# An attention kernel fused with a feed-forward layer: where batch index 0 forms phi's products for batch index 1

## The chip, the cores and the metric

The kernel runs on one core of a Trainium2 chip. The metric is device time in microseconds (us); all times without a unit are microseconds. TensorE (PE) multiplies matrices, VectorE (DVE) and ScalarE (ACT) do the elementwise work, and SyncE (SP) issues nearly all transfers (DMAs). PEld in the profile is PE's loading of weights, which overlaps its multiplying.

## The reference

Eight batches, eight heads, 576 tokens, head size 64, and 32 memory slots per head:

```python
a = phi - np.max(phi, axis=2, keepdims=True)
a = np.exp(a)
a = a / (np.sum(a, axis=2, keepdims=True) + 1e-09)
k_m = np.einsum('bhsm,bhsd->bhmd', a, k)
v_m = np.einsum('bhsm,bhsd->bhmd', a, v)
scores = scale * np.matmul(q, k_m.transpose(0, 1, 3, 2))
attn = softmax(scores)                  # over the 32 memory slots
x = np.matmul(attn, v_m)                # to (tokens, 512)
h = x @ w_in                            # 512 -> 2048
g = h * (1.0 / (1.0 + np.exp(-h)))
out = g @ w_out                         # 2048 -> 512
```

## The kernel before

**Stages of one batch.** The phi logits are reduced to their maximum, subtracted and exponentiated. `e_mm` (L325) multiplies them with a tile that holds k, v and a column of ones: four chunks of 128 tokens (L335, 32 products) and one of 64 (L345, 8 products). These are *phi's products*. Their result is 129 columns wide in two banks of PSUM, one per half of the heads. Behind them DVE adds an epsilon to the sums (L353) and inverts them (L355), and ACT (L359) and DVE (L361) write the scaled k_m and v_m, `kvn`. PE transposes that (`e_tr`, L367), makes the scores (`s_mm`, L400), and DVE and ACT do the softmax. x is never formed: `p_mm` (L649) multiplies v_m into w_in and gives *P*, and the FFN's first product is attention times P. In batch index 0, P is made in eight blocks of 256 columns; the sixth is `j == 5`. `p_split` (L677 on ACT, L679 on DVE) stores each block of P as a high and a low part.

**The FFN.** Batch indices 0 and 1 run 16 *slots*, one for each 128 columns of the hidden layer (L1300). In a slot, `ffn1` (L701, twelve products, high and low parts) writes h, two banks with 288 used columns each. ACT applies silu: L728 takes 512 tokens into `gbuf`, L730 the 64 others into `gleft`. DVE splits the result into high (L718) and low (L720) parts. Then PE does the second FFN product of the slot before, `main_step` (L746): four token tiles of three products each, into four accumulating banks. In batch index 0 the tiles go in two halves, and small steps ("events") stand behind each half: those of slot 8 behind tiles 0 and 1, those of slot 8.5 behind tiles 2 and 3.

**PSUM.** Eight banks: four accumulate (`acc`), two hold h, and two are the tile `bg`. Both have one buffer, so a new h or a new bg waits until all readers of the last are done. P's blocks and the scores use bg. Of h only columns 0 to 287 of each bank are used by the FFN; `beside_h` (L216) hands out columns from 288 on of the h in use.

**What sets the order.** PE's and SP's instructions stay in the order of the code. On ACT and DVE the framework orders batch index 0; the code adds that ACT's part of an event stands behind the last L730 (L1321). Each engine works its row strictly in order. Batch index 0 also converts the weights, from 64-bit words as they are loaded into the parts that the products need: per block of w_in or w_out, L172, L174 and L180 on ACT, and L176, L178 and L182 on DVE (`w_conv`). SP loads one block whenever another is done.

Of the kernel before, what the change touches and what calls it, by code (L numbers as in the profile page):

```python
# [23 lines left out]
KVW = 2 * D + 1  # L24
DMODEL, DFF = 512, 2048
NFC = DFF // P
CW = 256
# [21 lines left out]
def attn_ffn_kernel(  # L49
# [65 lines left out]
    def bgtile():  # L115
        return ps.tile([P, 2, 512], F32, tag="bg", name="bg", bufs=1)
# [90 lines left out]
    at = [dict() for _ in range(B)]  # L207
    live = {}

    def banks(b):  # L210
        if b == 0:
            return [ps.tile([P, 512], F32, tag="acc", name=f"first{i}", bufs=NI) for i in range(2)]
        bg = bgtile()
        return [bg[:, 0], bg[:, 1]]

    def beside_h(w):  # L216

        return [live["h"][:, i, HALF : HALF + w] for i in range(2)]
# [29 lines left out]
    def rows(p):  # L248
        return slice(REST * p, REST * (p + 1))
# [75 lines left out]
    def e_mm(b, cs=range(FULLC)):  # L325
        e, er, kvt, kr = (at[b][k] for k in ("e", "er", "kv", "kr"))
        if cs[0] == 0:
            at[b]["pt"] = beside_h(KVW) if b and b % 2 == 0 else banks(b)
        pt = at[b]["pt"]
        turns = [(c, p) for c in cs for p in range(2)]  # L330
        if b == 0:
            turns.sort(key=lambda t: t[1])
        for c, p in turns:
            for r in range(NR):
                nc.tensor.matmul(  # L335
                    pt[p][M * r : M * (r + 1), :KVW],
                    e[:, p, c, M * r : M * (r + 1)],
                    kvt[c][:, p, r],
                    start=c == 0, stop=False, skip_group_check=True,
                )  # L340
        if cs[-1] != FULLC - 1:
            return
        for r in range(NR):
            for p in range(2):
                nc.tensor.matmul(  # L345
                    pt[p][M * r : M * (r + 1), :KVW],
                    er[rows(p), M * r : M * (r + 1)],
                    kr[rows(p), r],
                    start=False, stop=True, skip_group_check=True,
                )  # L350
        rs = [sb.tile([P, 1], F32, tag="rs", name="rs", bufs=2) for p in range(2)]
        for p in range(2):
            nc.vector.tensor_scalar(rs[p], pt[p][:, 2 * D : KVW], EPS, None, op0=ALU.add)  # L353
        for p in range(2):
            nc.vector.reciprocal(rs[p], rs[p])  # L355
        for p in range(2):
            src = pt[p][:, : 2 * D].rearrange("p (k d) -> p k d", k=2)
            if p == (b == 0):
                nc.scalar.activation(kvn[:, :, p], src, AF.Copy, scale=rs[p])  # L359
            else:  # L360
                last_kvn[:] = [nc.vector.tensor_scalar(kvn[:, :, p], src, rs[p], None, op0=ALU.mult)]  # L361
# [656 lines left out]
    def ev(b, slot, fn, *a):  # L1018
        events.setdefault((b, slot), []).append((fn, a))

    def steady(b, n):


        early = b > 2
        if not early:
            ev(b, 1, phi_max, n)
            for i in range(3):
                ev(b, 2, phi_fold, n, i)
            ev(b, 3, phi_sub, n)
        ex = exp_slots(b)[0]  # L1030
        em = ex + 1 + b % 2
        ev(b, ex, phi_exp, n)
        ev(b, em, e_mm, n)
        for hf in range(2):
            ev(b, em + 1, load_q, n, hf)
        ev(b, ex + 4, e_tr, n)
        ev(b, ex + 5, s_all, n)
        ev(b, 9 if early else 10, s_max, n, ALL)
        ev(b, 10, s_sub, n, ALL)
        ev(b, 11, s_exp, n, ALL)  # L1040
        ev(b, 12 if early else 11, s_sum, n, ALL)
        ev(b, 13 if early else 12, s_norm, n, FIRST)
        turn = NFC + 3 if b % 2 else 14 if early else 13
        ev(b, turn, s_back, n, FIRST)
        ev(b, turn, s_high, n, FIRST)
        ev(b, turn, s_low, n, FIRST)
        for k in range(3):
            ev(b, 10 + 2 * k, win_load, n, k)
        if b % 2:
            ev(b, NFC, win_load, n, 3)  # L1050
        for k in range(2):
            ev(b, NFC + 2 if b % 2 else 13 + k, p_mm, n, k * JW, JW, True, b % 2 and k)
        m = n + 1
        if m < B:
            ev(b, ex + 3, load_kv, m, range(2))
            ev(b, ex + 3, load_phi, m)
            ev(b, ex + 6, load_kv, m, range(2, FULLC))
            ev(b, 7 if early else 14, phi_max, m)
            for i in range(3):
                ev(*((b, 11 + i) if early else (b + i // 2, (14, 15, 0)[i])), phi_fold, m, i, load)  # L1060
            ev(b + 1, 1, phi_sub, m)

    for b in range(B):
        n = b + 1
        if b == 0:
            for j in range(2, DFF // CW):
                ev(b, 2 * j - 1.5, p_mm, b, j * CW, CW)
        elif b == 1:
            ev(b, 0, win_save)
            for j in range(1, NJ):  # L1070
                ev(b, 4 * j - 3, p_mm, b, j * JW, JW)
            for j in range(NP):
                ev(b, 1.5 * j + 2, w_forms, j, 0)
                ev(b, 1.5 * j + 2.5, w_forms, j, 1)
        else:
            pair = b > 2 and b % 2 == 0
            if not pair:
                ev(b, 0, win_load, b, 3)
            ev(b, 0 if b > 2 else 1, p_mm, b, 2 * JW, JW)
            if b > 2:  # L1080
                ev(b, 3, s_norm, b, SECOND)
                for fn in (s_back, s_high, s_low):
                    ev(b, 4 + b % 2, fn, b, SECOND)
            late = b % 2 and 2 < b < B - 1
            ev(b, 0 if pair else 4 if late else 2, p_mm, b, 3 * JW, JW, not late, pair)
            if n < B:
                steady(b, n)
            if late:
                ev(b, 4, p_rest, b, 3 * JW)
            continue  # L1090
        at_slot = (
            (4, 5, 6, 7.5, 9, 9.5, 11.5, 12.5, 13, 13.5, 14, 14) if b == 0
            else (1, 2, 3, 5, 9, 10, 10, 11, 12, 13, 13, 14)
        )
        mx, sub, ex, em, tr, s0, s1, sx, se, ss, sn, sk = at_slot
        ev(b, mx, phi_max, n)
        if n == 1:
            ev(b, sub, phi_allmax, n, (0, 1), (0,))
            ev(b, sub + 0.5, phi_allmax, n, (0, 1), (1,))
        else:  # L1100
            for i in range(3):
                ev(b, sub, phi_fold, n, i)
        ev(b, sub + 0.5, phi_sub, n)
        ev(b, ex, phi_exp, n)
        ev(b, em, e_mm, n)
        ev(b, 14 if b == 0 else em + 1, load_kv, n + 1, range(FULLC if b == 0 else 2))
        ev(b, tr, e_tr, n)
        ev(b, em, load_q, n, 1)
        if n == 1:
            ev(b, s0, s_mm, n, 0)  # L1110
            ev(b, s1, s_mm, n, 1)
        else:
            ev(b, s0, s_all, n)
        if b == 0:
            ev(b, s1, load_q, n + 1, 0)
        else:
            ev(b, s1 + 1, load_kv, n + 1, range(2, FULLC))
        ev(b, sx, s_max, n, ALL)
        ev(b, sx, s_sub, n, ALL)
        ev(b, se, s_exp, n, ALL)  # L1120
        ev(b, ss, s_sum, n, ALL)
        ev(b, sn, s_norm, n, ALL)
        for u in (FIRST, SECOND) if n == 1 else (ALL,):
            ev(b, sk, s_back, n, ALL, u)
            ev(b, sk, s_high, n, ALL, u)
        ev(b, sk, s_low, n, ALL)
        ev(b, sk, load_phi, n + 1)
        if b == 0:
            ev(b, 14, p_mm, n, 0, JW)
        else:  # L1130
            for k in range(3):
                ev(b, 12 if k == 2 else 6 + k, win_load, n, k)
            for k in range(2):
                ev(b, 12 + 2 * k, p_mm, n, k * JW, JW)
# [17 lines left out]
    with in_order(DVE, ACT) as last:  # L1152
# [18 lines left out]
        for p in range(2):  # L1171
            phi_exp(0, (p,))
        keep_warm(idle, 2)
        e_mm(0)
        w_conv(I0, 0, "pc")
        keep_warm(idle, 3)
# [112 lines left out]
    for b in range(B):  # L1289
# [3 lines left out]
        for s in range(NFC if b > 1 else 0):  # L1293
            t, j = divmod(s, NP)
# [43 lines left out]
def build(arrays, bacc, num_devices=1):  # L1338
    nc = bacc.Bacc("TRN2", target_bir_lowering=False, num_devices=1, dynamic_dma_scratch_size=1024)
    aps = [  # L1340
        nc.dram_tensor(n, a.shape, mybir.dt.from_np(a.dtype), kind="ExternalInput").ap() for n, a in arrays.items()
    ]
    out = nc.dram_tensor("out", (B * S, DMODEL), F32, kind="ExternalOutput").ap()
    with tile.TileContext(nc) as tc:
        attn_ffn_kernel(tc, *aps, out)
    return nc
# [44 lines left out]
```

## Time and profile before

| | |
|---|---|
| median of 3 runs | 679.05 (678.32 to 679.21) |
| the profiled execution | 678.47, of it span 676.7 |
| PE busy | 667.1 (99%) |
| PE weight loads busy | 588.6 (87%) |
| DVE busy | 518.6 (77%) |
| ACT busy | 368.5 (54%) |
| transfers | 93.92 MB |
| PE's granted clock, mean | 0.999 |

The span runs from the first instruction to the last. The times in rows of the profile count from its start. A row of a timeline has start, duration, engine, line, operation, what it writes and reads, and in brackets how long the engine stood idle ahead of it and what ended that. Matmuls are pipelined: the step from start to start is what one costs, and the duration holds the way through the array too. Batch index 0 ends at about 105 of 676.7.

### The profile page before, as it was taken

The page shows a single profiled execution, that of the slowest core. Times are in us where ns is not written, and L with a number is a line of the kernel's source. Part 1 is how long each engine was busy: PE and PEld are TensorE (multiplying, and loading weights), DVE is VectorE, ACT ScalarE, POOL GpSimd, SP SyncE. Part 2 cuts the span into 40 slices and gives each one's busy share as a digit, 9 for nine tenths or more (in the row PEclk, how much of TensorE's full clock was granted, in tenths as well). Part 3 has the DMA queues.
Part 4 walks back from the last instruction along what each step waited for, and adds up shares of the span by engine and source line. Part 5 has one row for each costly group of instructions (what it writes and reads, how often), then busy time and mean ns, then how long its engine had stood idle before and what let it go on. Part 6 is the DMA issues. An engine that isn't in the chain of part 4 may idle for free.

```text
span 676.7 us, 14541 instructions
## 1 busy us (share of the span) xinstructions
PE 667.1 (99%) x5792; PEld 588.6 (87%) x5792; DVE 518.6 (77%) x1093; ACT 368.5 (54%) x681; POOL 0.7 (0%) x6
## 2 busy tenths in 40 slices
PE   7999999999999999999999999999999999999997
PEld 3577778787888998999988999899997999889996
DVE  4997899988948689868877688877877668867653
ACT  3878684533625556654655546564654546554541
POOL 0000000000000000000000000000000000000000
PEclk9999999999999999999999999999999999999999
DMA  9998975224270552253420535116430204300001
GB/s 340 373 339 276 315 304 192 81 103 146 78 233 22 184 183 100 79 180 124 179 95 16 185 97 179 70 42 237 157 126 32 86 2 156 111 31 17 32 1 47
DMA packets 37907, 93.92 MB, mean 139 GB/s; under 512 B 4688, under 2 KB 21456, under 8 KB 34256
## 3 DMA queue, kind: packets, MB, share of 16 engines
q1 hardware_dynamic: 36816, 90.22, 38.4%
q10 hardware_dynamic: 1024, 2.77, 1.1%
q8 instruction: 46, 0.75, 0.5%
q14 instruction: 21, 0.17, 0.1%
HBM read 77.22 MB, written 15.73 MB: 137 GB/s over the span
## 4 chain that ended last, share of the span: by engine, by line
PE 73%; DVE 10%; issue 2%; ACT 2%; DVEq 0%; ACTq 0%
PE sum L893 35%; PE h L854 22%; PE lsum L977 5%; PE bg L649 3%; PE acc L746 3%; PE h L701 2%; PE accleft L746 2%; DVE gparts L720 1%; PE bg L335 1%; PE bg L382 1%; DVE pm L679 1%; DVE kept L836 1%; DVE gparts L718 1%; DVE smx L426 1%; PE h L335 1%
## 5 line engine op out<-in xcount | busy, mean ns | idle before, releaser
L854 PE MATMUL h<-aparts,pm 128*128 128x288 f32 x1152 | 168.7, 295 | 0.0
L854 PEld LDWEIGHTS h<-aparts,pm 128*128 128x128 f32 x1152 | 157.3, 188 | 0.8
L868 ACT ACTIVATE gbuf<-h 128x512 f32<-128x512 f32 x96 | 57.3, 597 | 117.0 <-PE h L854 113.7
L893 PE MATMUL sum<-wo_hi,aparts 128*128 128x256 f32 x384 | 102.6, 289 | 0.0
L893 PE MATMUL sum<-kept,aparts 128*128 128x256 f32 x576 | 100.1, 282 | 0.0
L893 PE MATMUL sum<-wo_lo,aparts 128*128 128x256 f32 x384 | 100.0, 282 | 0.0
L873 DVE TENSOR_TENSOR gbuf<-gbuf 128x256 f32<-128x256 f32 x96 | 40.5, 422 | 71.4 <-ACT gbuf L868 70.9
L882 ACT ACTIVATE aparts<-gbuf 128x512 fp32r<-128x512 f32 x86 | 54.4, 633 | 63.4 <-DVE gbuf L877 63.4
L746 PE MATMUL acc<-wo_hi,gparts 128*128 128x512 f32 x256 | 85.0, 397 | 0.2
L893 PEld LDWEIGHTS sum<-wo_hi,aparts 128*128 128x128 f32 x384 | 72.8, 189 | 11.5 <-ACT gleft L870 10.1
L893 PEld LDWEIGHTS sum<-kept,aparts 128*128 128x128 f32 x576 | 82.6, 191 | 0.0
L884 DVE TENSOR_TENSOR gparts<-gbuf,aparts 128x512 fp32r<-128x512 f32 x86 | 59.5, 692 | 19.1 <-ACT aparts L882 19.1
L893 PE MATMUL sum<-wo_hi,gparts 128*128 128x256 f32 x384 | 73.2, 281 | 0.0
L893 PEld LDWEIGHTS sum<-wo_lo,aparts 128*128 128x128 f32 x384 | 73.1, 190 | 0.0
L893 PE MATMUL sum<-kept,gparts 128*128 128x256 f32 x288 | 65.5, 282 | 0.0
L746 PEld LDWEIGHTS acc<-wo_hi,gparts 128*128 128x128 f32 x256 | 47.6, 188 | 14.5 <-DVE gparts L720 1.5
L893 PEld LDWEIGHTS sum<-wo_hi,gparts 128*128 128x128 f32 x384 | 59.4, 190 | 0.0
L701 PEld LDWEIGHTS h<-aparts,pm 128*128 128x128 f32 x372 | 51.7, 188 | 6.8 <-issue 3.4
L701 PE MATMUL h<-aparts,pm 128*128 128x288 f32 x372 | 56.0, 299 | 0.6 <-DVE aparts L612 0.5
L872 ACT ACTIVATE aparts<-gbuf 128x384 fp32r<-128x384 f32 x96 | 50.4, 525 | 0.0
L746 PE MATMUL acc<-wo_lo,gparts 128*128 128x512 f32 x128 | 49.3, 393 | 0.4 <-DVE wo_lo L182 0.4
L893 PEld LDWEIGHTS sum<-kept,gparts 128*128 128x128 f32 x288 | 47.9, 190 | 0.0
(225 smaller groups left out, 956.1 us busy)
## 6 DMA issues: line engine op xcount, KB each, us to landing
win<-win_saved SPq DMA_DIRECT2D x24, 1024.0 KB, 5.2
kv<-in_kv SPq DMA_DIRECT2D x28, 516.0 KB, 5.0
q<-in_q SPq DMA_DIRECT2D x16, 576.0 KB, 6.2
raw<-in_w_in SPq DMA_DIRECT2D x14, 512.0 KB, 7.6
raw<-in_w_out SPq DMA_DIRECT2D x6, 1024.0 KB, 6.5
win_saved<-win SPq DMA_DIRECT2D x4, 1024.0 KB, 8.6
phi<-in_phi SPq DMA_DIRECT2D x7, 576.0 KB, 8.3
out<-oo SPq DMA_DIRECT2D x26, 128.0 KB, 2.3
```

The costliest lines, as they stand in the source:

```text
L335: nc.tensor.matmul(pt[p][M * r : M * (r + 1), :KVW], e[:, p, c, M * r : M * (r + 1)], kvt[c][:, p, r], start=c == 0, stop=False, skip_grou ...
L649: nc.tensor.matmul((bg[p][M * r : M * (r + 1)] if beside else bg[M * r : M * (r + 1), p, :w]).rearrange("p (k f) -> p k f", f=P), kvT[D * ...
L701: nc.tensor.matmul(h[:, hf, :HALF], wt[:, p, fs], a[:, p, hf * HALF : (hf + 1) * HALF], start=n[hf] == 0, stop=n[hf] == 5, skip_group_chec ...
L746: nc.tensor.matmul(acc[key], gt[:, cs], wt[:, fc], start=fc == 0 and n == 0, stop=fc == NFC - 1 and n == 2)
L854: nc.tensor.matmul(h[:, i, :HALF], wt[:, p, f : f + P], a[:, p], start=n == 0, stop=n == 5)
L868: nc.scalar.activation(gbuf[:, :MAIN].rearrange("p (i f) -> p i f", i=2), h[:, :, :w], AF.Silu)
L872: nc.scalar.activation(hi[:, :3], g[:, 1:4], AF.Copy)
L873: nc.vector.tensor_tensor(g[:, 4:6], g[:, :1].broadcast_to([P, 2, P]), g[:, 1:3], op=ALU.subtract)
L882: nc.scalar.activation(hi[:, 3:], g[:, 4:], AF.Copy)
L884: last_split.append(nc.vector.tensor_tensor(lo[:, 3:], g[:, 4:], hi[:, 3:], op=ALU.subtract))
L893: nc.tensor.matmul(sums[bank][:, place * Q : (place + 1) * Q], gt[:, k], wt, start=bank not in begun, stop=True, skip_group_check=True,)
L977: nc.tensor.matmul(sums[k], part[gt][:, 2 * i + k], wt[:, fc], start=n == 0 and i == 0 and m == 0, stop=True, skip_group_check=True,)
```

## The change

It concerns batch index 0 alone, where phi's products for batch index 1 are made. They move from slot 7.5, behind tiles 2 and 3, to slot 8, behind tiles 0 and 1, and write beside h instead of into bg. P's sixth block moves from slot 8.5 to slot 8 and stands just ahead of them. The load of the second half of batch index 1's q is tied to the same slot and moves along.

```diff
     def e_mm(b, cs=range(FULLC)):
         e, er, kvt, kr = (at[b][k] for k in ("e", "er", "kv", "kr"))
         if cs[0] == 0:
-            at[b]["pt"] = beside_h(KVW) if b and b % 2 == 0 else banks(b)
+            at[b]["pt"] = beside_h(KVW) if b == 1 or b and b % 2 == 0 else banks(b)
...
         if b == 0:
             for j in range(2, DFF // CW):
-                ev(b, 2 * j - 1.5, p_mm, b, j * CW, CW)
+                ev(b, 8 if j == 5 else 2 * j - 1.5, p_mm, b, j * CW, CW)
...
         at_slot = (
-            (4, 5, 6, 7.5, 9, 9.5, 11.5, 12.5, 13, 13.5, 14, 14) if b == 0
+            (4, 5, 6, 8, 9, 9.5, 11.5, 12.5, 13, 13.5, 14, 14) if b == 0
             else (1, 2, 3, 5, 9, 10, 10, 11, 12, 13, 13, 14)
         )
         mx, sub, ex, em, tr, s0, s1, sx, se, ss, sn, sk = at_slot
```

PE before, from the last product of slot 6 (written in slot 7) to slot 8's first FFN product (L701):

```order
L746 MATMUL acc_419<-wo_hi,gparts 128x512
L335 MATMUL bg<-kv_0_438,phi_431 32x129 x8
L335 MATMUL bg<-kv_1_440,phi_431 32x129 x8
L335 MATMUL bg<-kv_2_442,phi_431 32x129 x8
L335 MATMUL bg<-kv_3_444,phi_431 32x129 x8
L345 MATMUL bg<-kr_446,phi_431 32x129 x8
L701 MATMUL h<-aparts,pm 128x288 x12
```

PE now, in slot 8, from tile 1 to tile 2 of slot 7's second product:

```order
L746 MATMUL acc_397<-wo_hi,gparts 128x512
L649 MATMUL bg<-win_74,kvT_224 32x256 x8
L335 MATMUL h<-kv_0_438,phi_431 32x129 x8
L335 MATMUL h<-kv_1_440,phi_431 32x129 x8
L335 MATMUL h<-kv_2_442,phi_431 32x129 x8
L335 MATMUL h<-kv_3_444,phi_431 32x129 x8
L345 MATMUL h<-kr_446,phi_431 32x129 x8
L746 MATMUL acc_417<-wo_hi,gparts 128x512
```

Where phi's products stood, slot 8's L701 now follows the L746 at once. The products have moved behind it and half a `main_step`, behind P's sixth block (L649), and write h. Behind them come six L746 and slot 9's L701, which writes the next h.

ACT before, from the last step of a w_in and w_out conversion (L174) to slot 9's silu (the second L728); in brackets the engines that an instruction waits for:

```order
L174 ACTIVATE raw<-raw 128x1024
L180 ACTIVATE wo_hi<-cva 128x1024 [waits DVE_49]
L359 ACTIVATE kvn<-bg,rs 128x2x64 [waits DVE_49,PE_49]
L728 ACTIVATE gbuf<-h 128x512 [waits PE_49]
L730 ACTIVATE gleft<-h 128x64
L677 ACTIVATE pm<-bg 128x2x256 [waits PE_49]
L728 ACTIVATE gbuf<-h 128x512 [waits PE_49,Activation_49]
```

ACT now, the same place:

```order
L174 ACTIVATE raw<-raw 128x1024
L728 ACTIVATE gbuf<-h 128x512 [waits PE_49]
L180 ACTIVATE wo_hi<-cva 128x1024 [waits DVE_49]
L730 ACTIVATE gleft<-h 128x64
L677 ACTIVATE pm<-bg 128x2x256 [waits PE_49]
L359 ACTIVATE kvn<-h,rs 128x2x64 [waits DVE_49,PE_49]
L728 ACTIVATE gbuf<-h 128x512 [waits PE_49,Activation_49]
```

Slot 8's L728 has come ahead of the conversion's L180, its L730 stands behind that L180, and L359 has gone behind both and behind P's L677.

SP's row at the loads of the last two blocks of w_out (raw) and of q, before (-) and now (+); q_1_780 and q_1_822 are the second half of batch index 1's q:

```order
 L88 DMA raw<-in_w_in 128x4x128 x2
-L88 DMA raw<-in_w_out 128x2x512
-L88 DMA q_1_780<-in_q 128x1152
-L88 DMA raw<-in_w_out 128x2x512
-L88 DMA q_0_973<-in_q 128x1152
+L88 DMA raw<-in_w_out 128x2x512 x2
+L88 DMA q_1_822<-in_q 128x1152
+L88 DMA q_0_972<-in_q 128x1152
```

The load of q has gone behind the last load of w_out.

## The prediction

> **What bounds the kernel now.** I read the page's busy table first, then the chain of waits, then the timelines of TensorE (PE), ScalarE (ACT) and VectorE (DVE) around the place that the change touches. The page:
>
> ```profile
> span 676.7 us, 14541 instructions
> PE 667.1 (99%) x5792; PEld 588.6 (87%) x5792; DVE 518.6 (77%) x1093; ACT 368.5 (54%) x681; POOL 0.7 (0%) x6
> ```
>
> PE is busy for 99% of the span. Whatever makes PE stand still is lost, unless a later stall shrinks in return. So I follow PE through the stretch, in absolute times of this execution. Its timeline, with start, duration, instruction, and idle time ahead:
>
> ```profile
> 60.30 0.50 PE L746 MATMUL acc<-wo_lo,gparts 128*128 128x512 f32 x1 [0.44 <-DVE wo_lo L182]
> 62.68 0.39 PE L746 MATMUL acc<-wo_hi,gparts 128*128 128x512 f32 x1
> 63.00 1.97 PE L335 MATMUL bg<-kv,phi 128*32 128x129 f32 x64
> 64.90 0.45 PE L345 MATMUL bg<-kr,phi 64*32 64x129 f32 x16
> 65.28 1.87 PE L701 MATMUL h<-aparts,pm 128*128 128x288 f32 x12
> 66.98 0.39 PE L746 MATMUL acc<-wo_hi,gparts 128*128 128x512 f32 x1
> 69.50 0.39 PE L746 MATMUL acc<-wo_hi,gparts 128*128 128x512 f32 x1
> 69.82 0.66 PE L649 MATMUL bg<-win,kvT 64*32 64x256 f32 x16
> 70.41 1.87 PE L701 MATMUL h<-aparts,pm 128*128 128x288 f32 x12
> ```
>
> From 63.00 on these follow each other without a stall: phi's products (L335, L345) take 65.28 - 63.00 = 2.28, slot 8's first FFN product (L701) 65.28 to 66.98 = 1.70, the twelve products of the second FFN step (L746) 66.98 to 69.50, 11 steps of 0.23, P's sixth block (L649) 70.41 - 69.82 = 0.59. Now ACT in the same stretch:
>
> ```profile
> 62.93 0.60 ACT L728 ACTIVATE gbuf<-h 128x512 f32<-128x512 f32 x1
> 63.42 0.22 ACT L730 ACTIVATE gleft<-h 128x64 f32<-128x64 f32 x1
> 66.72 1.14 ACT L174 ACTIVATE raw<-raw 128x1024 int32<-128x1024 uint32 x1
> 67.82 1.06 ACT L180 ACTIVATE wo_hi<-cva 128x1024 fp32r<-128x1024 f32 x1
> 68.79 0.34 ACT L359 ACTIVATE kvn<-bg,rs 128x128 f32<-128x128 f32 x1
> 69.03 0.59 ACT L728 ACTIVATE gbuf<-h 128x512 f32<-128x512 f32 x1
> 69.51 0.22 ACT L730 ACTIVATE gleft<-h 128x64 f32<-128x64 f32 x1
> 61.64:69.51 7.87, 7.86 (x11) 1.00 0.65 174
> ```
>
> The last row is ACT's busy time in a stretch, 7.86 of 7.87. The reader should see that ACT is behind and has no gap: slot 8's silu (L728, L730) starts at 69.03, though its product ended on PE at 65.28 + 1.87 = 67.15. Slot 7's silu starts as late as 62.93. PE does not notice, because it has other work: at 63.00 that work is phi's products.
>
> **The change part by part.** It removes no instruction and adds none; what moves is shown in the section on the change.
>
> *Phi's products leave their old place.* PE is free at 62.68 + 0.23 = 62.91, and slot 8's product is now next. It writes h, so it needs slot 7's L730, which ends at 63.42 + 0.22 = 63.64. A release takes about 0.05: the DVE row below ends at 59.02 + 1.23 = 60.25, and L746 starts at 60.30. So it starts at 63.69, and PE loses 0.78. The 2.28 of phi's products were the cover. It also needs the low part of P's fifth block, which DVE has at 61.65 + 0.69 = 62.34, in time.
>
> ```profile
> 59.02 1.23 DVE L182 TENSOR_TENSOR wo_lo<-raw,wo_hi 128x1024 fp32r<-128x1024 f32 x1
> 61.65 0.69 DVE L679 TENSOR_TENSOR pm<-bg,pm 128x512 fp32r<-128x512 f32 x1 [1.41 <-ACT pm L677]
> 65.82 1.23 DVE L178 CUSTOM_DVE_ANT_0 win<-raw,win 128x2048 uint16<-128x2048 uint16 x1 [0.36 <-ACT raw L174]
> ```
>
> *P's sixth block comes half a step earlier.* Product 1.70 and six L746 (6 x 0.23 = 1.38) bring PE to 66.77, and with the 0.09 of a change of shape (62.91 to 63.00) to 66.86. The block reads win, which L178 finishes at 67.05, so it starts at 67.10: 0.24 lost. Before, the block came 2.8 later than L178. It ends at 67.69.
>
> *Phi's products beside h.* They now write columns 288 to 416 of the two banks of h, which slot 8's silu reads in columns 0 to 287. There is such a case in the trace, batch index 2's products in batch index 1's slot 5 (PEld is PE's weight loads):
>
> ```profile
> 131.81 0.22 ACT L730 ACTIVATE gleft<-h 128x64 f32<-128x64 f32 x1
> 132.16 1.70 PEld L335 LDWEIGHTS h<-kv,phi 128*32 128x32 f32 x64 [0.84 <-ACT gleft L730]
> 134.44 0.50 PE L746 MATMUL acc<-wo_hi,gparts 128*128 128x512 f32 x1
> 134.78 0.39 PE L746 MATMUL acc<-wo_lo,gparts 128*128 128x512 f32 x1
> ```
>
> The view names L730 as the releaser: it ended at 132.03, the products began at 132.16. The built program says the same of the new place: the ACT count that L335 waits for is the one that slot 8's own L730 reaches. ACT gets there by adding rows: L174 gives way at 67.82; the silu now comes first, 69.51 - 69.03 = 0.48; then L180, 68.79 - 67.82 = 0.97; then L730, 0.22. That is 69.49, and with the release 69.54. PE has waited since 67.69: 1.85 lost, the largest term. Nothing shortens it, since ACT has no gap from 61.64 on, and the silu before it, slot 7's, is where it was. By address the wait would not be needed, and then this term would be 0. [...]
>
> *The next h.* Products 2.28, to 71.82; six L746 with 0.11 extra after the change of shape (134.44 to 134.78 is 0.34 where a step is 0.23), 1.49, to 73.31. Slot 9's product needs all readers of h gone, DVE's L353, L355, L361 and ACT's L359. In batch index 1 that chain took:
>
> ```profile
> 136.05 0.21 DVE L353 TENSOR_SCALAR rs<-h 128x1 f32<-128x1 f32 x2
> 137.57 1.48 PEld L701 LDWEIGHTS h<-aparts,pm 128*128 128x128 f32 x11 [0.54 <-DVE kvn L361]
> ```
>
> So 1.52 from L353 to the released product. The last of phi's products is out 0.07 after PE moves on (64.90 + 0.45 against 65.28), and 0.10 for DVE to start gives 71.99 + 1.52 = 73.51: 0.20 lost. Slot 9's product was at 70.41 and will be at 73.51: **3.10 late**. The losses add up to the same: 0.78 + 0.24 + 1.85 + 0.20 = 3.07, and 0.03 of changes of shape. Even if the terms 0.24 and 0.20 vanish, ACT alone gives 69.54 + 2.28 + 1.49 = 73.31, so 2.90. A gain here is excluded by ACT's row of work.
>
> *Behind it all moves by 3.10*, because ACT's conversions stand behind a silu that waits for PE:
>
> ```profile
> 82.94 0.60 ACT L728 ACTIVATE gbuf<-h 128x512 f32<-128x512 f32 x1 [1.19 <-PE h L701]
> 83.54 1.15 ACT L172 ACTIVATE win<-raw 128x1024 f32<-128x1024 f32 x1
> ```
>
> *The load of q's second half* moves with the products' event and in SP's queue falls behind w_out's last load. SP's queue, the DMA answers for it and for a lone phi load, the scores that read q (L400), and the L182 that frees the buffer:
>
> ```profile
> 76.46 0.37 SPq L88 DMA_DIRECT2D raw<-in_w_out  x1
> 76.87 0.47 SPq L88 DMA_DIRECT2D q<-in_q  x1
> 80.54 0.37 SPq L88 DMA_DIRECT2D raw<-in_w_out  x1
> DMA to landing us min/median/max: 6.3/6.8/7.3
> phi<-in_phi SPq DMA_DIRECT2D x1, 576.0 KB, 3.8
> 79.26 1.22 DVE L182 TENSOR_TENSOR wo_lo<-raw,wo_hi 128x1024 fp32r<-128x1024 f32 x1
> 85.52 0.72 PE L400 MATMUL bg<-q,kvT 64*32 64x288 f32 x16
> ```
>
> The 6.3 is of the load at 76.46, the 7.3 of the one at 76.87, so they landed at 82.8 and 84.2: 576 KB cost 1.4, and 1024 KB by that 2.5. The last w_out load follows L182 (80.48, issued 80.54); shifted it is issued at 83.64, q 0.41 behind it. A lone 576 KB took 3.8, so 2.4 without the transfer; 2.4 + 2.5 + 1.4 = 6.3 puts q at 89.95. L400 wants it at 85.52 + 3.10 = 88.62: 1.35 lost with the release. Bounds: q alone, 3.8 after its issue at 84.05, is in time (0); with the 7.3 of a crowded queue it is 91.35 (2.8). I take 1.35, since the load ahead is there in any case.
>
> *What is given back.* The chain of waits runs on DVE from 87.60 to 108.06, its first piece here, and PE's loads stall at its end:
>
> ```profile
> 87.60 0.76 DVE sc L412 x2
> 108.06 0.30 PEld L746 LDWEIGHTS acc<-wo_hi,gparts 128*128 128x128 f32 x2 [0.50 <-DVE gparts L720]
> ```
>
> While PE waits for q, DVE works on, so the stall of 0.50 goes, some 0.4 of it PE's own. If q is on time, DVE sets this point: there L178 now stands ahead of L412 and waits for its L174, which costs up to 0.4, and nothing is given back.
>
> Sum: 3.10 + 1.35 - 0.4 = **4.05**. The profiled execution took 678.47 and would take 682.5. The median of the three runs is 679.05, 0.58 above it, so the median should be **683.1**. About 0.2% (1.36) is what a measurement of this kernel can tell from no change.
>
> **The rivals.**
> 1. *The waits at h, and q late* (as above): 683.1, chance 0.70.
> 2. *The waits at h, q in time.* For it: 3.8 for a lone load. Then 3.10 + 0.4 = 3.5: 682.55. Chance 0.18.
> 3. *Not slower: the lost time is absorbed by the DVE chain.* If the DVE row of work from 87.60 to 108.06 hung on loads and conversions that do not move, PE could lose 3.10 earlier and still arrive at 108.06, and the 0.1 or so of the saved change of shape is left: 679.0. The point that decides is whether L172 at 83.54 starts 3.10 later. Against it: its L728 waits for PE, 1.19 in the row. Chance 0.06, of which I give a third to a gain above 0.2%.
> 4. *The clock falls in the pause.* If PE's granted clock halved after the 1.85, the products and six L746 behind it, 2.28 + 1.38, would take twice as long: 683.1 + 3.7 = 686.8. [...] The trace has the PE at a granted clock of 1.00 throughout, with 1.35 idle at the start at most:
>
> ```profile
> 0.00:4.00 4.00, 2.65 (x7) 0.99 (x8) 0.00 (x0) 1.49 (x2) 0.70 (x6) 1.00 0.53 155
> ```
>
> (The 1.00 behind the five engines is the clock.) Chance 0.06.
>
> **The numbers.** Cases 1, 2 and 4 are slower, 0.94; case 3 gives 0.04 the same and 0.02 faster. The range: below, ACT's bound 2.90 on the fastest run shown, 678.32, gives 681.2, and I go to 681.0 for the give-back; above, q at its upper end, 3.10 + 2.8 - 0.4 = 5.5 on 679.21 gives 684.7, rounded to 685.0. Left out are cases 3 and 4, 0.12, and some of what is off in the durations.
>
> **What would show it.** In the profile after: L701 of slot 8 idle for some 0.8 behind ACT gleft L730; L335 in h idle for some 1.9 behind gleft L730, starting near 69.5; L701 of slot 9 near 73.5, released by kvn L361; L400 on the second half of q waiting 0 to 2.8 for a DMA; the stall of 108.06 gone where q waits. Wrong would be: L335 in h starting before 69, or slot 9's product before 73.3, or a span that differs by less than 1.4 with these waits present.

## The result, and the profile after

| | before | changed |
|---|---|---|
| median | 678.8 (678.26 to 679.34, 6 runs) | 683.1 (681.91 to 683.87, 6 runs) |
| the profiled execution | 678.47, span 676.7 | 682.77, span 681.0 |
| granted clock, mean | 0.999 | 0.999 |

The changed kernel is slower: ratio 1.0063, 95% interval 1.005 to 1.0076. The page of the changed kernel:

```profile
span 681.0 us, 14543 instructions
PE 666.8 (98%) x5792; PEld 588.6 (86%) x5792; DVE 518.8 (76%) x1093; ACT 368.8 (54%) x681; POOL 0.7 (0%) x6
```

PE does the same work (666.8 against 667.1), and each engine of the page runs as many instructions as before; the 4.3 by which the span is longer are idle time. To compare the two timelines a common point is needed, and the absolute times are not one: slot 7's first product, ahead of all that the change touches, starts at 57.75 before and at 58.28 now. First three L701 of the kernel before: slot 7's, the one behind q's scores (L400 on the second half of q), and one behind the stall of 108:

```profile
57.75 1.87 PE L701 MATMUL h<-aparts,pm 128*128 128x288 f32 x12
86.16 1.87 PE L701 MATMUL h<-aparts,pm 128*128 128x288 f32 x12
110.50 1.75 PE L701 MATMUL h<-aparts,pm 128*128 128x288 f32 x12
```

Then PE's timeline of the changed kernel, with the same three among its rows (here and below, rows between those shown are left out, mostly L746, also where no dots stand):

```profile
58.28 1.87 PE L701 MATMUL h<-aparts,pm 128*128 128x288 f32 x12
...
63.25 0.39 PE L746 MATMUL acc<-wo_hi,gparts 128*128 128x512 f32 x1
64.23 1.87 PE L701 MATMUL h<-aparts,pm 128*128 128x288 f32 x12 [0.59 <-ACT gleft L730]
67.59 0.67 PE L649 MATMUL bg<-win,kvT 64*32 64x256 f32 x16
69.97 1.97 PE L335 MATMUL h<-kv,phi 128*32 128x129 f32 x64 [1.71 <-ACT gleft L730]
73.75 1.80 PE L701 MATMUL h<-aparts,pm 128*128 128x288 f32 x12
90.50 0.72 PE L400 MATMUL bg<-q,kvT 64*32 64x288 f32 x16 [1.66 <-DMA q<-in_q]
91.15 1.86 PE L701 MATMUL h<-aparts,pm 128*128 128x288 f32 x12
...
114.96 1.75 PE L701 MATMUL h<-aparts,pm 128*128 128x288 f32 x12
```

Slot 9's product went from 70.41 to 73.75; less the 0.53 of the common point it is 2.81 late. The L701 behind q's scores went from 86.16 to 91.15, which by the same count is 4.46 late, q's pause included; that of 110.50 stands at 114.96, 3.93 late. So the loss is made in two places, phi's products and q, and a part of it is given back near 108. The rest of the span takes and gives a few tenths more, which I have not followed.

ACT's timeline shows why phi's products started no sooner:

```profile
67.17 1.20 ACT L174 ACTIVATE raw<-raw 128x1024 int32<-128x1024 uint32 x1
68.24 0.62 ACT L728 ACTIVATE gbuf<-h 128x512 f32<-128x512 f32 x1
68.72 1.08 ACT L180 ACTIVATE wo_hi<-cva 128x1024 fp32r<-128x1024 f32 x1
69.66 0.25 ACT L730 ACTIVATE gleft<-h 128x64 f32<-128x64 f32 x1
```

L730 ends at 69.91, the products begin at 69.97. Slot 8's product is out at 64.23 + 1.87 = 66.10; between it and them lie the end of ACT's backlog (the last L174 is shown), the silu, and all of L180. SP's queue shows the load of q, where x2 joins two loads of one kind; the second w_out load took 0.37, so it was issued at 79.72 + 4.47 - 0.37 = 83.82, and q 0.42 behind it:

```profile
79.72 4.47 SPq L88 DMA_DIRECT2D raw<-in_w_out  x2
84.24 0.94 SPq L88 DMA_DIRECT2D q<-in_q  x2
```

The answer for that q load gives 6.1 from issue to landing, so it landed near 90.3, and L400 started at 90.50.

One more view, the windows of 2 around both pauses (busy time of PE, PEld, DVE, ACT and POOL, then the granted clock, then the DMA share and GB/s):

```profile
68.00:70.00 2.00, 0.29 (x19) 0.03 (x5) 1.74 (x4) 2.00 (x5) 0.00 (x0) 1.00 0.71 74
88.00:90.00 2.00, 0.85 (x4) 0.38 (x2) 1.67 (x2) 2.00 (x3) 0.00 (x0) 1.00 1.04 425
```

The clock stays at 1.00 in both. This execution says nothing of the others, though: the six took 681.91, 682.73 and 682.77 at a mean clock of 0.998 or 0.999, and 683.43, 683.65 and 683.87 at 0.997. That split has to be explained as well.

### The profile page after: what moved, and what is told of

It is laid out like the page before. It is cut to its first block, busy times and chain, and to the rows that moved or that the text cites. A ratio compares the mean times of both kernels' runs of the same rounds, so it can differ in the third digit from the quotient of the medians.

```text
span 681.0 us, 14543 instructions
## 1 busy us (share of the span) xinstructions
PE 666.8 (98%) x5792; PEld 588.6 (86%) x5792; DVE 518.8 (76%) x1093; ACT 368.8 (54%) x681; POOL 0.7 (0%) x6
## 4 chain that ended last, share of the span: by engine, by line
PE 79%; DVE 6%; ACT 4%; issue 1%; DMA 1%; SPq 0%; DVEq 0%; ACTq 0%
PE sum L893 32%; PE h L854 20%; PE acc L746 8%; PE lsum L977 5%; PE h L701 5%; PE bg L649 3%; PE accleft L746 2%; PE h L335 1%; PE bg L382 1%; DMA q<-in_q 1%; PE bg L335 1%; ACT aparts L882 1%; DVE gbuf L873 1%; PE pacc L649 1%; ACT raw L174 0%
## 5 line engine op out<-in xcount | busy, mean ns | idle before, releaser
L746 PE MATMUL acc<-wo_hi,gparts 128*128 128x512 f32 x256 | 85.3, 397 | 0.1
L746 PEld LDWEIGHTS acc<-wo_hi,gparts 128*128 128x128 f32 x256 | 47.7, 188 | 14.1 <-DVE t L836 1.7
L701 PEld LDWEIGHTS h<-aparts,pm 128*128 128x128 f32 x372 | 51.8, 188 | 6.9 <-issue 1.9
L701 PE MATMUL h<-aparts,pm 128*128 128x288 f32 x372 | 55.7, 298 | 1.1 <-ACT gleft L730 0.6
L746 PE MATMUL acc<-wo_lo,gparts 128*128 128x512 f32 x128 | 49.3, 392 | 0.4 <-DVE wo_lo L182 0.4
```

The lines of the kernel that those rows point to most:

```text
L701: nc.tensor.matmul(h[:, hf, :HALF], wt[:, p, fs], a[:, p, hf * HALF : (hf + 1) * HALF], start=n[hf] == 0, stop=n[hf] == 5, skip_group_chec ...
L746: nc.tensor.matmul(acc[key], gt[:, cs], wt[:, fc], start=fc == 0 and n == 0, stop=fc == NFC - 1 and n == 2)
```

## The experiments

Theory 1 is the prediction's: PE waits at h, since its cover is gone and ACT's backlog stands ahead of L730, and it waits for q, which is loaded behind w_out. Theory 2 came up with the first results: in some executions the clock falls behind one of these pauses. In the diffs below the kernel that is edited is the changed one, unless the text says otherwise.

**The load of q early again.**

```diff
-        ev(b, em, load_q, n, 1)
+        ev(b, 7.5 if b == 0 else em, load_q, n, 1)
```

> Changed kernel, with the load of q's second half alone put back to half a step earlier, ahead of w_out's last load. Theory 1 (the waits at h, and q late): L400 on q's second half starts without a wait for a DMA, so its 1.7 goes; the stall near 108 on gparts L720, which had gone, comes back with some 0.5. Slot 9's product stays 2.8 late against slot 7's. Time about 1.1 below the changed kernel's 683.1, at 682.0 (681.5 to 682.5), still some 3 above the kernel before. Rival (the load is hidden by a wait that would come anyway, the scores' chain on VectorE): another wait of the same length stands where L400 waited, and the time stays at 683.1, within 0.4.

Measured: 681.33 (680.59 to 683.34, 5 runs), ratio to the kernel before 1.0039 (1.0026 to 1.0051). Its slot 7 starts at 58.27, so its times can be laid beside those of the changed kernel directly. PE's scores, then PE's weight loads near the old stall:

```profile
88.78 0.71 PE L400 MATMUL bg<-q,kvT 64*32 64x288 f32 x16
```

```profile
111.32 0.30 PEld L746 LDWEIGHTS acc<-wo_hi,gparts 128*128 128x128 f32 x2 [0.51 <-DVE gparts L720]
```

L400 has no idle time ahead of it and stands at 88.78 instead of 90.50: the pause at q was 1.72. The stall that was at 108.06 before is back, with 0.51. So q is worth 1.72 - 0.51 = 1.2, and the rival, that another wait would have taken its place, is out. The time is 0.2 under the range expected, which was counted from the median of 683.1. Slot 9's product is at 73.72 here, 73.75 there: the load has no part in the first loss. One of the five executions took 683.34, at a clock of 0.997.

**The load of q late, alone** (an edit of the kernel before).

```diff
-        ev(b, em, load_q, n, 1)
+        ev(b, 8 if b == 0 else em, load_q, n, 1)
```

> Kernel before, with the load of q's second half alone moved behind w_out's last load; phi's products and P's block stay where they were. Theory 1: w_out's last load is issued at 80.5, q at about 80.95, and it lands 6.1 (as in the changed kernel) to 7.6 later, at 87.0 to 88.5, while L400 wants it at 85.5: a stall of 1.5 to 3.0, of which about 0.5 comes back at the stall of 108.06. Time 1.0 to 2.5 above the kernel before, 679.8 to 681.3. Rival (q is late only because PE's delay pushes the loads together): no stall at L400, time within 0.3 of the kernel before.

Measured: 682.24 (680.66 to 683.76, 5 runs), ratio 1.0046 (1.0032 to 1.006). PE's timeline, and windows over the same place:

```profile
88.22 0.72 PE L400 MATMUL bg<-q,kvT 64*32 64x288 f32 x16 [2.61 <-DMA q<-in_q]
88.88 3.25 PE L701 MATMUL h<-aparts,pm 128*128 128x288 f32 x12
```

```profile
86.00:88.00 2.00, 0.00 (x0) 0.00 (x0) 1.79 (x3) 2.00 (x3) 0.00 (x0) 1.00 1.02 419
88.00:89.00 1.00, 0.78 (x17) 0.34 (x17) 1.00 (x1) 0.72 (x1) 0.00 (x0) 0.91 1.03 419
89.00:92.00 3.00, 3.00 (x13) 3.00 (x14) 1.99 (x4) 0.00 (x0) 0.00 (x0) 0.50 1.03 395
92.00:93.00 1.00, 1.00 (x5) 0.82 (x5) 0.15 (x1) 0.78 (x3) 0.00 (x0) 0.88 0.97 293
```

The pause came as expected, 2.61 within 1.5 to 3.0, with all of phi's products at their old place: it is the order in SP's queue that makes q late. What I had not expected stands in the next row: the twelve products of L701 took 3.25 instead of 1.87, and the clock was 0.50 from 88.8 to 92.2 (0.91 in a window of 1 is 0.18 of it at half speed, 0.88 is 0.24), 3.4 in all. That is theory 2, seen for the first time. The two executions with a clock of 0.999 or 1.000 took 680.66 and 681.27, inside the 679.8 to 681.3 expected; the three at 0.996 or 0.997 took 682.24 to 683.76.

**Slot 8's L730 ahead of L180.** The last step of one w_out block's conversion, L180 and L182, moves behind phi's products:

```diff
-        ev(0, slot, conv_next, *(("pc",) if len(to_do) == 1 else ()))
+        o4 = slot == 7.5
+        ev(0, slot, conv_next, *(("pc",) if len(to_do) == 1 else ("pcsa",) if o4 else ()))
+        if o4:
+            ev(0, 8, w_conv, ("o", 4), None, "hl")
```

> Changed kernel, with the last step of one w_out block's conversion (ScalarE's L180 of 0.97 and VectorE's L182 of 1.23) moved behind phi's products, so that slot 8's L730 does not stand behind L180. Theory 1: L335 in h waits for L730 behind ScalarE's backlog, so its wait of 1.79 falls by 0.8 to 1.0 and the products start near 69.0 instead of 69.97; the rest of the timeline follows 0.9 earlier unless L182, which now stands behind the kvn chain, makes L746 wait for its weights. Time about 0.9 below the changed kernel, 682.2 (681.8 to 682.8). Rival (the products wait for something that ScalarE's order does not set, as the bank's own work or the weights): the wait stays at 1.8 and the time at 683.1.

Measured: 681.12 (680.66 to 681.8, 5 runs), ratio 1.0032 (1.0019 to 1.0044). ACT's timeline and PE's, from its slot 7 at 58.03 on:

```profile
67.97 0.60 ACT L728 ACTIVATE gbuf<-h 128x512 f32<-128x512 f32 x1
68.45 0.23 ACT L730 ACTIVATE gleft<-h 128x64 f32<-128x64 f32 x1
...
69.03 1.08 ACT L180 ACTIVATE wo_hi<-cva 128x1024 fp32r<-128x1024 f32 x1
```

```profile
68.74 1.97 PE L335 MATMUL h<-kv,phi 128*32 128x129 f32 x64 [0.75 <-ACT gleft L730]
```

L730 now ends at 68.68, and the products start 0.06 behind it. The pause fell from 1.71 to 0.75, by one L180, and slot 9's product stands 72.51 - 58.03 = 14.48 behind slot 7's, where the changed kernel has 15.47. So it is ACT's row of work that sets the start of phi's products. The time is 1.1 lower than expected, and 0.65 of that belongs to theory 2: I had counted from a median of 683.1, in which half of the executions had a lower clock (without them it is 682.45, see below), and here none of the five has (all 1.000).

The pause ahead of L400 was 1.45 here. That is no effect of this edit, since the changed kernel's four profiles have 1.66, 1.46, 1.53 and 1.50. In seven of the nine profiles with such a pause the row names DVE's conversion of win (L178) as what ended it, and not q, since the two come within 0.1 of each other. L178 is not the cause: with q early, L400 starts at 88.78, while that L178 runs from 89.02 to 90.25. In all nine, q lands about 0.1 before L400 starts.

**Both edits together.**

> Changed kernel with both edits: the load of q's second half early, and the last conversion step of one w_out block behind phi's products. Theory 1: the two gains are of different waits and add up but for what VectorE's chain near 108 takes back: slot 9's product some 1.9 late instead of 2.8, no wait at L400, time 681.0 (680.5 to 681.5), some 2 above the kernel before. Rival (both waits hide one behind the other, so that one edit gives what both give): 682.0 or more.

Measured: 680.23 (679.62 to 680.7, 11 runs), ratio 1.0017 (1.0008 to 1.0026), no execution below a clock of 0.999. By the medians the two edits nearly add up: the changed kernel's executions without a fall of the clock have a median of 682.45 (all its runs of this study), those of the two single edits 681.17 and 681.12, so each takes 1.3 and both take 2.2, where a plain sum would be 2.6. The timelines, which are free of the start-up, do add up. From slot 7's L701 to the one near 114 the changed kernel's four profiles take 56.47 to 56.68, q early 55.49, L730 early 55.61, both 54.50: about 1.0, 0.9 and 2.0 less. The time is 0.3 under the range expected. This is the best of the changed versions, and it is still slower than the kernel before: with its slot 8 waiting 0.61 and phi's products 0.74, waits that the kernel before does not have.

**The changed kernel once more.**

> The changed kernel once more, unchanged. In the runs so far its time fell into two groups, 681.9 to 682.8 at a mean granted clock of 0.998 or 0.999, and 683.4 to 683.9 at 0.997. Theory 2 (beside the waits, the granted clock falls to half behind one of PE's pauses in a part of the executions): the runs form two groups again, with the clock 0.002 to 0.003 lower in the longer one, and where the profiled execution is of that group a stretch of about 3.3 at a clock of 0.50 stands right behind the pause at h (1.8) or at q (1.7). Rival (the second group is noise of other causes, DMA or start-up): no link between clock and time, and a profile of the longer group has 1.00 in every stretch from 58 to 130.

Measured: 682.74 (682.22 to 684.76, 5 runs), ratio 1.0067 (1.0053 to 1.0081). Again two groups: 682.22, 682.6 and 682.74 at 0.999 or 1.000, then 683.76 at 0.997 and 684.76 at 0.996. The profiled one was of the first group.

**P's sixth block back at its old place.**

```diff
-                ev(b, 8 if j == 5 else 2 * j - 1.5, p_mm, b, j * CW, CW)
+                ev(b, 2 * j - 1.5, p_mm, b, j * CW, CW)
```

> Changed kernel, with P's sixth block back at its old place, half a step behind the products beside h. Theory 1: the products wait for slot 8's L730 as before, but the block is no longer ahead of them to fill 0.6 of it: the pause ahead of L335 in h grows from 1.8 to 2.5 (and the 0.18 for win goes), and slot 9's product stands about 0.6 later than in the changed kernel, so that 683.3 to 683.7 without a fall of the clock. By theory 2 a pause of 2.5 drops the clock in half of the executions or more, which adds 1 to 2: 685. Rival (the block moved ahead is itself a cost, and the kernel gets faster when it goes back): 682.5 or less.

Measured: 684.31 (683.0 to 684.84, 5 runs), ratio 1.0079 (1.0066 to 1.0091). The profiled execution, the one of 683.0, has on PE:

```profile
69.83 1.97 PE L335 MATMUL h<-kv,phi 128*32 128x129 f32 x64 [2.44 <-ACT gleft L730]
```

The pause grew from 1.71 to 2.44, as the block's 0.6 no longer fills it. Slot 9's product stands 74.29 - 58.21 = 16.08 behind slot 7's, 0.61 more than in the changed kernel, as expected. Without a fall of the clock the kernel takes 683.0 (here) and 683.06 (below), against 682.45 of the changed one: the block's move is the part of the change that saves time. Three of the five had a clock of 0.996 and one 0.998.

**Phi's products in slot 8, but in bg.**

```diff
-            at[b]["pt"] = beside_h(KVW) if b == 1 or b and b % 2 == 0 else banks(b)
+            at[b]["pt"] = beside_h(KVW) if b and b % 2 == 0 else banks(b)
...
-                ev(b, 8 if j == 5 else 2 * j - 1.5, p_mm, b, j * CW, CW)
+                ev(b, 2 * j - 1.5, p_mm, b, j * CW, CW)
```

> Changed kernel, with phi's products in slot 8 but in bg as before, not beside h, so that P's sixth block comes behind them again. Theory 1: L701 of slot 8 still loses 0.75, the products no longer wait for slot 8's L730 (start near 67.5 where the changed kernel has 69.97), but P's block, which writes bg too, now waits for the kvn chain, which stands on VectorE behind L182: L353 near 71.4, block near 72.7, a pause of about 1.6; slot 9's product near 73.4, 0.3 earlier than in the changed kernel; q late as before. Time 682.7 (682 to 683.5). Rival (the place beside h is the whole cost): slot 9's product near 71.8, time 681 or less.

Measured: 681.89 (681.72 to 682.43, 5 runs), ratio 1.0047 (1.0034 to 1.0059). PE's timeline, from its slot 7 at 57.73 on:

```profile
63.67 1.87 PE L701 MATMUL h<-aparts,pm 128*128 128x288 f32 x12 [0.60 <-ACT gleft L730]
66.85 1.97 PE L335 MATMUL bg<-kv,phi 128*32 128x129 f32 x64
...
72.34 0.67 PE L649 MATMUL bg<-win,kvT 64*32 64x256 f32 x16 [1.55 <-DVE kvn L361]
```

In bg the products wait for nothing, and the pause moves on to P's block, which needs the bg that they filled: 1.55, as expected 1.6. Slot 9's product is 0.26 earlier than in the changed kernel (0.3 expected); the time is just under the range expected. The place beside h is thus not the whole cost. Whichever bank is used, somebody stands behind the products' readers, half a step after them.

**Phi's products beside h at their old place** (an edit of the kernel before).

```diff
-            at[b]["pt"] = beside_h(KVW) if b and b % 2 == 0 else banks(b)
+            at[b]["pt"] = beside_h(KVW) if b == 1 or b and b % 2 == 0 else banks(b)
```

> Kernel before, with phi's products beside h but at their old place half a step earlier, ahead of slot 8's L701; the load of q and P's block as before. Theory 1: the products wait for slot 7's L730 (0.75), and slot 8's L701, which now stands right behind them and needs h, waits for the whole kvn chain: L361 ends near 69.5, so L701 starts at 69.4 to 69.8 instead of 65.28 and PE pauses 3.5 to 4; q in time; slot 9's product 4.2 later, 0.5 back at the stall of 108. Without a fall of the clock 682.6; by theory 2 a pause of that length drops the clock to 0.50 in every execution, some 1.7 more: 684.3. Rival (with q in time and no product delayed behind the silu of slot 8, the place beside h costs under 1): 679.8 or less.

Measured: 684.98 (684.57 to 685.38, 4 runs), ratio 1.0091 (1.0077 to 1.0105). PE's timeline, and DVE's:

```profile
64.22 1.97 PE L335 MATMUL h<-kv,phi 128*32 128x129 f32 x64 [0.63 <-ACT gleft L730]
66.11 0.45 PE L345 MATMUL h<-kr,phi 64*32 64x129 f32 x16
70.14 3.25 PE L701 MATMUL h<-aparts,pm 128*128 128x288 f32 x12 [3.58 <-DVE kvn L361]
```

```profile
67.54 0.22 DVE L353 TENSOR_SCALAR rs<-h 128x1 f32<-128x1 f32 x2
...
68.48 1.23 DVE L178 CUSTOM_DVE_ANT_0 raw<-raw,cva 128x2048 uint16<-128x2048 uint16 x1
69.74 0.35 DVE L361 TENSOR_SCALAR kvn<-h,rs 128x128 f32<-128x128 f32 x1
```

L701 of slot 8 needs the h in which the products lie and waits 3.58 for L361, with conversions ahead of it on DVE. Behind that pause its twelve products took 3.25: the clock fell here too. Of the four executions three stood at 0.996; the fourth, at 0.998, was the longest.

**Three more profiles, for the place of the fall.**

> The changed kernel, one look for a profile of an execution in which the clock falls (5 of 11 so far by their clock of 0.996 or 0.997, and none of them the profiled one). Theory 2: if this one is 683.4 or longer, its profile has a clock of 0.50 over about 3.3, behind the pause of 1.8 at h or behind that of 1.7 at q; if the fall is at h, the six L746 and slot 9's L701 take twice their time there, and the pause at q gets shorter, since q does not wait for PE. If it is 682.8 or less, the clock is 1.00 in every stretch. Rival (the longer executions have other causes): a time of 683.4 or more with a clock of 1.00 throughout.

> The same once more, with the same expectations: 683.4 or more with a clock of 0.50 behind one of the two pauses, or 682.8 or less with 1.00 throughout. Rival: 683.4 or more with 1.00 throughout.

> The changed kernel with P's sixth block back at its old place, one look for the same purpose (its pause at h is 2.4, and 3 of its 5 executions had a clock of 0.996). Theory 2: at 684 or more, the clock is 0.50 for about 3.3 from the products beside h on, which then take some 4 instead of 2.3; at 683.0 it is 1.00 throughout. Rival: 684 or more with 1.00 behind the pause at h, the fall standing elsewhere or nowhere.

Measured: 681.76, 682.3 and 683.06, at a clock of 0.999, 1.000 and 0.999. None of the three had a fall, so they tell nothing of its place.

**A pause at h alone, of 2.4**: P's block at its old place and the load of q early, by the two edits shown above.

> The changed kernel with two edits: P's sixth block back at its old place (the pause ahead of phi's products in h is then 2.4, not 1.8), and the load of q's second half early again (no pause at q). Theory 1 without a fall of the clock: 683.0 of the first edit alone, less some 1.3 for q, 681.7 at a clock of 0.999 or 1.000. Theory 2a (the clock falls behind the pause at h): 2 to 4 of the 5 executions have a clock of 0.996 to 0.998 and take 683 to 684. Theory 2b (it falls behind the pause at q): no execution has a clock under 0.999, and all are 681.2 to 682.2.

Measured: 683.36 (682.48 to 683.59, 5 runs), ratio 1.0058 (1.0044 to 1.0073). One execution took 682.48 at 0.999, the four others 683.19 to 683.59 at 0.997. The profiled one is of the four; PE's timeline and the windows:

```profile
69.53 3.61 PE L335 MATMUL h<-kv,phi 128*32 128x129 f32 x64 [2.43 <-ACT gleft L730]
73.07 0.45 PE L345 MATMUL h<-kr,phi 64*32 64x129 f32 x16
```

```profile
67.00:69.00 2.00, 0.10 (x1) 0.00 (x0) 1.77 (x3) 2.00 (x3) 0.00 (x0) 1.00 0.33 60
69.00:70.00 1.00, 0.47 (x12) 0.43 (x16) 1.00 (x3) 0.48 (x2) 0.00 (x0) 0.77 0.78 139
70.00:73.00 3.00, 3.00 (x60) 2.52 (x52) 1.27 (x2) 0.00 (x0) 0.00 (x0) 0.51 1.00 322
73.00:74.00 1.00, 1.00 (x22) 0.67 (x19) 0.30 (x4) 0.00 (x0) 0.00 (x0) 1.00 1.04 438
```

The 64 products of phi took 3.61 instead of 1.97 at half the clock, 1.64 more. Theory 2b, that only the pause at q does it, is out: the pause at h is enough, as the one at q was when it stood alone. L400 had no idle time here, and PE's next longest pause behind the start-up was 0.63. The execution without a fall took 682.48, 0.8 more than expected without one, which I cannot explain.

Counted over all executions, with the pauses of the profiled one:

| kernel | pause at h, or at P's block | pause at q | executions | clock 0.997 or less |
|---|---|---|---|---|
| both edits | 0.74 | none | 11 | 0 |
| L730 early | 0.75 | 1.45 | 5 | 0 |
| products in bg | 1.55 | 1.51 | 5 | 0 |
| q early | 1.72 | none | 5 | 1 |
| changed kernel | 1.71 | 1.66 | 13 | 5 |
| P's block late, q early | 2.43 | none | 5 | 4 |
| P's block late | 2.44 | 1.48 | 6 | 3 |
| q late alone | none | 2.61 | 5 | 3 |
| products beside h, old place | 3.58 | none | 4 | 3 |

The falls of this table are told by the mean clock; seen in a profile are three, behind 2.43, 2.61 and 3.58. The kernel before had 0.999 or 1.000 in each of its 15 executions beside the first four experiments, and of the 18 beside the others. A fall shows in the mean: 3.4 at half the clock is 3.4 x 0.5 / 681 = 0.0025. But the mean also holds the tail behind PE's last product, where the clock falls too: 0.80 at half speed in the trace of the kernel before, and 2.04 in the changed kernel's first profile, which costs 0.0015. So 0.998 alone decides nothing. The three executions at 0.998 are 681.91 of the changed kernel, among its shortest, and 684.52 and 685.38 of the kernels with 2.44 and 3.58, long like those with a fall.

## Why the prediction was right, and where it was not

**The sum of the waits.** By the prediction's own steps, with what the changed kernel's trace shows:

- *Slot 8's L701 behind slot 7's L730:* 0.78 predicted. PE was free at 63.25 + 0.23 = 63.48 and started at 64.23: 0.75.
- *P's block behind win:* 0.24 predicted. Free at 64.23 + 1.70 + 1.38 + 0.09 = 67.40, started at 67.59: 0.19.
- *Phi's products behind slot 8's L730:* 1.85 predicted. Free at 67.59 + 0.59 = 68.18, started at 69.97: 1.79. The edit that brought L730 forward shows the cause and not only the size.
- *Slot 9's L701 behind the kvn chain:* 0.20 predicted, nothing measured. 69.97 + 2.28 + 1.49 = 73.74, it started at 73.75. The 1.52 of batch index 1 was too long a chain for this place: from L353 at 72.42 to the end of L361 it took 1.21. Here PE's six L746 are what ended last.
- *Slot 9's product:* 3.10 late predicted, 2.81 measured. That is under the 2.90 which the prediction held for ACT's bound, and by the common point the product stands at 73.22, narrowly on the wrong side of its own sign of 73.3. ACT came 0.11 earlier than added up: L730 ended at 69.91 - 0.53 = 69.38 instead of 69.49.
- *The pause at q:* 1.35 predicted, 1.72 measured against the kernel with q early. The landing was as worked out: 6.5 behind the issue of the w_out load ahead (83.82 to 90.3) instead of 6.3. The term is larger because PE came earlier.
- *Given back near 108:* 0.4 predicted; the L701 rows give 4.46 - 3.93 = 0.53, and 0.51 is what returned when q was in time.
- *Sum:* 4.05 predicted, 3.93 in the timeline up to 115.

**The rivals.** The second, q in time, was out of the question as soon as q stood behind w_out: alone it paused PE for 2.61. The third, that DVE's chain absorbs the loss, fell with the first timeline: ACT's L172, at 83.54 before, starts at 86.80, which is 2.73 later by the common point, so the chain moved along. The fourth, the falling clock, got a chance of 0.06, and that is the step which failed: it was my estimate, from a trace in which no pause ahead of PE's last product is longer than 1.35, and no run had shown what a pause of 1.85 does. In the three profiles with a fall the clock went to 0.50 behind pauses of 2.43, 2.61 and 3.58. By the mean clock, pauses of 1.7 were followed by a fall in 6 of 18 executions, of 2.4 in 7 of 11, of 2.6 in 3 of 5.

The clock of 1.00 throughout, on which that estimate leaned, was misread too. In the trace of the kernel before, the clock falls to 0.50 at 675.89, 3.17 after PE's last product. And at the start PE's first ten products (L80) follow each other by 0.43, three of the same shape from 6.94 on by 0.22, so by my estimate from these steps the clock was about half there. The view shows 1.00, since the trace has no record of the clock ahead of 6.88.

Its price was off in the other direction. The prediction let the fall last for all of phi's products and six L746, 3.7; it ended after 3.4 at half speed in each of the three profiles, which made phi's products 1.64 longer where the fall lay on them (3.61 instead of 1.97). In the changed kernel the 8 executions without a fall have a median of 682.45 and the 5 with one 683.76, so it costs 1.3 there. Rival 4 as written, 686.8 in the median, did not come; a fall of the clock there was, by the mean clock, in 5 of 13 executions.

**So the number is right for two reasons, not one.** Without a fall the kernel is 682.45 - 678.8 = 3.65 slower, a little less than the 4.05 predicted, and the executions with a fall lift the median of the first six to 683.1, of all 13 to 682.74. That the first median met the prediction to the tenth is chance.

**What stays open.** Which of the two pauses drops the clock in the changed kernel was not caught in a profile. With q early the pause at h is the only one of that length, and one execution of five stood at 0.997 and took 683.34; of the ten executions whose longest pause was 1.45 to 1.55 none did. That speaks for h, but so few executions do not show it. Whether phi's products would be safe beside h without the wait for L730 was not tried.

## What to carry to other kernels

Work that looks movable may be the cover of the wait ahead of the instruction that moves up: before moving it, read what the engine would wait for without it, and where the thing that it now needs stands in the other engine's row. Follow every load that is tied to the moved step through its queue; here a third of the loss was one DMA that fell behind a larger one. And when executions of one kernel fall into two groups, compare the mean granted clock first: behind a pause of 1.7 on PE another 1.3 was lost in some of them.

## What the runs showed of the hardware

**Behind some pauses on PE the clock fell to 0.50 for 3.4.** Three profiles have a fall inside the run. Its start and its length are worked out from the clock of the windows; for the products beside h that is 0.79, 0.50 and 0.86 in the windows from 69 to 71, 71 to 73 and 73 to 75, and for the two others it is in the rows shown above.

| profile | pause on PE | PE goes on at | the clock falls to 0.50 at | for |
|---|---|---|---|---|
| products beside h, old place | 3.58 | 70.14 | 70.16 | 3.4 |
| q late alone | 2.61 | 88.22 | 88.82 | 3.4 |
| P's block late, q early | 2.43 | 69.53 | 69.54 | 3.4 |

A pause of the same length was not followed by a fall in each execution. Both profiles of P's block late have 2.44 at h, and phi's products behind it took 1.97 in both; the first shows 1.00 in every window from 56 to 130. The four profiles of the changed kernel have 1.70 to 1.72 at h, and the products took 1.97 there too. Behind PE's last product the clock fell again, after 3.17 in the trace of the kernel before and after 1.93 in the changed kernel's first. Why it falls behind a pause in one execution and not behind the same pause in another was not shown.

**The start-up differs from execution to execution.** In four profiles of the changed kernel slot 7's L701 started at 57.73, 58.05, 58.28 and 58.47. So 0.7 of difference between two profiles can be there before the change begins, and two traces are better compared from a common instruction on. The profile with 57.73, which is within 0.02 of the kernel before, has a span of 680.0, 3.3 longer than before.
